# Decay tables as eight rows spread by TensorE, one batch's decays on GpSimd, and fewer products of zeros at the start of a retention and feed-forward kernel

One core of one Trainium2 chip. The metric is the device time of a run in microseconds; the profile's span is 1.7 to 2.1 us shorter than that time in every run here. "Fast": a run within 1.5% of the fastest of its kernel. In the profiles PE is TensorE, PEld its weight loads, DVE VectorE, ACT ScalarE, POOL GpSimd, and SP the engine that issues the loads; a load has landed when its last byte has.

## The reference

```python
def _attn_ref(q, k, v):                       # batch 4, heads 8, sequence 768, head size 64
    gamma = 1.0 - 2.0 ** (-5.0 - np.arange(H, dtype=np.float32))
    scale = 1.0 / np.sqrt(D)
    for t in range(S):
        state = gamma[None, :, None, None] * state + np.einsum('bhd,bhe->bhde', k[:, :, t], v[:, :, t])
        y[:, :, t] = scale * np.einsum('bhd,bhde->bhe', q[:, :, t], state)

def _moe_ref(x, w_in, w_out):                 # 3072 x 512, w_in 512 x 2048, w_out 2048 x 512
    h = x @ w_in
    g = np.maximum(0.01 * h, h)
    return (g @ w_out).astype(np.float32)
```

The recurrence is done in chunks of 128 tokens (per chunk and batch: scores, mask, values, state). The decays of the heads come from a table that the host makes from the number of heads alone. The weights arrive as 64-bit floats in pieces of 512 KB, and ScalarE and VectorE turn each into fp32 before TensorE can use it.

## The kernel before

Only the opening matters here. The table lies in `dec`: 512 columns for the outputs (`gq`), 8 for the values (`gk`), 4 for the states (`gc`), all for 128 partitions.

```python
    dec = const.tile([128, HP * C + H + HP], FP32, name="dec")
    # ...
    def decay_v(c, b, engine=nc.gpsimd):          # values times gk
    def tokens_taken(c, b, xb):                   # outputs times gq, from PSUM into x; taken calls it
    # ...
    load_qk(0, 0)
    nc.sync.dma_start(out=dec[:, rates:], in_=decay[:, rates:])     # 6 KB in rows of 48 bytes
    load_v(0, 0)
    load_qk(0, 1)
    nc.sync.dma_start(out=dec[:, :rates], in_=decay[:, :rates])     # 256 KB
    load_v(0, 1)
    load_piece(0)                                 # first weight piece
    load_qk(0, 2)
    load_v(0, 2)
    load_piece(1)                                 # second weight piece
    # ...
    keep_busy(7)                                  # products of zeros, 128x128 by 128x512
    score(0, 0)
    masked(0, 0)
    decay_v(0, 0, nc.vector)
    keep_busy(6)
    score(0, 1)
    values(0, 0)
    masked(0, 1)
    decay_v(0, 1, nc.vector)
    keep_busy(3)
    next_powers()                                 # ScalarE's three steps on a weight piece
    taken(0, 0, x)
    values(0, 1)
    taken(0, 1, x)
    next_powers()
    next_mantissas()                              # VectorE's three steps: L339, L341, L343
    score(0, 2)
    keep_busy(3)
    steps = direct(0, 0, x, parts[0][1], 0)       # four steps, one for each weight piece
    next(steps)
    next_mantissas()
    # ...
```

The products of zeros have no use but to keep PE busy until data come.

Of the kernel before, what the change touches and what calls it, by code (L numbers as in the profile page):

```python
# [9 lines left out]
FP32 = mybir.dt.float32  # L10
U32 = mybir.dt.uint32
# [5 lines left out]
ALU = mybir.AluOpType  # L17

C = 128
W = 512  # L20
# [3 lines left out]
def kernel(  # L24
# [35 lines left out]
    nc = tc.nc  # L60
    NC = S // C
    DM = H * D
    HP = H // 2
    NU = DF // 512
    N = B * C // 2
    f64 = weights.dtype == I64
# [4 lines left out]
    psum = ctx.enter_context(  # L71
        tc.tile_pool(name="psum", bufs=2, space=bass.MemoryType.PSUM))

    mask = const.tile([128, 128], FP32, name="mask")
    dec = const.tile([128, HP * C + H + HP], FP32, name="dec")
# [17 lines left out]
    def new_pair(h):  # L93

        pairs = units.setdefault(N_UNITS - 1, [])
        if len(pairs) == h:
            pairs.append(work.tile([128, 2, 2, 256], FP32, tag="raw", bufs=3, name=f"last{h}"))
# [12 lines left out]
    gq = dec[:, 0 : HP * C].rearrange("p (j m t) -> p j m t", j=2, t=C)  # L110
    gk = dec[:, HP * C : HP * C + H]
    gc = dec[:, HP * C + H :]
# [5 lines left out]
    def place_for(c, b, place=None):  # L118

        if place is None:  # L120
            x = work.tile([128, 2, HP, C], FP32, tag="qk", bufs=AHEAD, name=f"qk_{c}_{b}")
            y = work.tile([128, 2, H, D], FP32, tag="kv", bufs=AHEAD, name=f"kv_{c}_{b}")
        else:
            flat = place.rearrange("p i k n -> p (i k n)")
            half = 2 * HP * C
            x = flat[:, 0:half].rearrange("p (s a t) -> p s a t", s=2, a=HP)
            y = flat[:, half : 2 * half].rearrange("p (s h d) -> p s h d", s=2, h=H)
        heads[c, b] = x, y

    def load_qk(c, b):  # L130
        nc.sync.dma_start(out=heads[c, b][0], in_=qk[c, b])
# [7 lines left out]
    def load(c, b, place=None):  # L139
        place_for(c, b, place)  # L140
        load_qk(c, b)
        nc.sync.dma_start(out=heads[c, b][1], in_=kv[c, b])

    def decay_v(c, b, engine=nc.gpsimd):
        v = heads[c, b][1][:, 1]
        if engine is not nc.scalar:
            engine.tensor_tensor(out=v, in0=v, in1=gk.unsqueeze(2).to_broadcast([128, H, D]),
                                 op=ALU.mult)
        else:
            for h in range(H):  # L150
                engine.activation(v[:, h], v[:, h], AF.Identity, scale=gk[:, h : h + 1])
# [3 lines left out]
    def two_banks(name):  # L155
        return psum.tile([128, 2, HP, C], FP32, tag="att", bufs=2, name=name)

    def score(c, b):

        x = heads[c, b][0]  # L160
        ps = scores[c, b] = two_banks(f"ap_{c}_{b}")
        for a in range(HP):
            for u in range(2):
                for j in range(2):
                    nc.tensor.matmul(ps[ts(u, 64), j, a, :], lhsT=x[ts(j, 64), 1, a, ts(u, 64)],  # L165
                                     rhs=x[ts(j, 64), 0, a, :])

    def masked(c, b):
        am = work.tile([128, 2, HP, C], FP32, tag="am", bufs=2, name=f"am_{c}_{b}")
        nc.vector.tensor_tensor(  # L170
            out=am.rearrange("p j a t -> p (j a) t"),
            in0=scores[c, b].rearrange("p j a t -> p (j a) t"),
            in1=mask.unsqueeze(1).to_broadcast([128, H, C]), op=ALU.mult)
        scores[c, b] = am
# [54 lines left out]
    def taken(c, b, xb):  # L229

        tokens_taken(c, b, xb)
        state_taken(c, b)

    def tokens_taken(c, b, xb):
        ps = sums_at[c, b]
        th, o = divmod(b * C, N)
        blocks = xb.rearrange("p (kh th) k n -> p kh th k n", th=2)[:, :, th, :, ds(o, C)]
        nc.vector.tensor_tensor(out=blocks, in0=ps[:, :, 0 : HP // 2, :], in1=gq, op=ALU.mult)  # L238

    def state_taken(c, b):  # L240
        ps = sums_at.pop((c, b))
        if 0 < c < NC - 1:
            nc.vector.tensor_tensor(out=st[b], in0=st[b], in1=for_state(ps), op=ALU.add)
            nc.vector.tensor_tensor(out=st[b], in0=st[b],
                                    in1=gc.unsqueeze(2).to_broadcast([128, HP, D]), op=ALU.mult)
# [17 lines left out]
    raws = {}  # L263
# [5 lines left out]
    def piece(n):  # L269

        k, h, i = n // 4, n // 2 % 2, n % 2
        if k < N_UNITS - 1:
            return unit(k)[:, 2 * h : 2 * h + 2, i, :]
        new_pair(h)
        return units[k][h][:, :, i, :]

    def load_piece(n, place=None):
        if n >= N_PIECES:
            return
        if not f64:  # L280
            nc.sync.dma_start(out=piece(n), in_=weights[n].rearrange("p (h n) -> p h n", h=2))
            return
        if place is None:
            tag, bufs = ("raw", 3) if n < N_PIECES - 4 else (("qk", "kv")[n % 2], AHEAD)
            raws[n] = work.tile([128, W], I64, tag=tag, bufs=bufs, name=f"raw{n}")
        else:
            raws[n] = place.bitcast(I64)
        nc.sync.dma_start(out=raws[n], in_=weights[n])
# [4 lines left out]
        if n < N_PIECES and f64:  # L293
            powers(n)

    def next_mantissas():
        n = done["mantissas"]
        done["mantissas"] += 1
        if f64:
            mantissas(n)  # L300
        if n != 3:
            load_piece(n + 4 if n < 3 else n + 3)
        if n == N_PIECES - 1:
            new_pair(2)
            for b in range(AHEAD):
                load(2, b)
        if n % 4 == 3 and n > 7:
            add_sums(n // 4)

    def round_piece():  # L310

        next_mantissas()
        next_powers()
# [17 lines left out]

    def mantissas(n):

        z = zs.pop(n)
        words = raws.pop(n).bitcast(U32).rearrange("p (h n two) -> p h n two", two=2, h=2)
        lo, hi = words[:, :, :, 0], words[:, :, :, 1]
        f = piece(n)
        m = f.bitcast(U32)
        nc.vector.tensor_scalar(out=m, in0=hi, scalar1=0x000FFFFF, scalar2=0x00100000,  # L339
                                op0=ALU.bitwise_and, op1=ALU.bitwise_or)  # L340
        nc.vector.scalar_tensor_tensor(out=f, in0=lo, scalar=2.0 ** -32, in1=m,  # L341
                                       op0=ALU.mult, op1=ALU.add)
        nc.vector.scalar_tensor_tensor(out=f, in0=f, scalar=2.0 ** -20, in1=z.bitcast(BF16),  # L343
                                       op0=ALU.mult, op1=ALU.mult)
# [175 lines left out]
    def tile_x(c):  # L520
        return work.tile([128, 4, 2, N], FP32, tag="x", bufs=2, name=f"x_{c}")

    def new_x(c):
        x = tile_x(c)
        t = work.tile([128, 3, 2, N], FP32, tag="t", bufs=2, name=f"t_{c}")
        return x, t

    def new_o(c):
        return work.tile([128, 4, 2, N], FP32, tag="o", bufs=2, name=f"o_{c}")
# [35 lines left out]
    def rounds(*steps):  # L565
        return {i: [round_piece] for i in steps}

    rates = HP * C
    place_for(0, 0)
    place_for(0, 1)  # L570
    place_for(0, 2, new_o("in2"))
    place_for(0, 3, new_o("in3"))
    load_qk(0, 0)
    nc.sync.dma_start(out=dec[:, rates:], in_=decay[:, rates:])
    load_v(0, 0)
    load_qk(0, 1)
    nc.sync.dma_start(out=dec[:, :rates], in_=decay[:, :rates])
    load_v(0, 1)
    load_piece(0)
    load_qk(0, 2)  # L580
    load_v(0, 2)
    load_piece(1)
    load_piece(2)
    load_piece(3, tile_x("words").rearrange("p i k n -> p (i k n)")[:, 0 : 2 * W])
    load_qk(0, 3)
    load_v(0, 3)
    for b in range(B):
# [6 lines left out]



    xs = {0: new_x(0)}
    os = {}
    parts = [new_g(0, 0)]
    x, t = xs[0]  # L600



# [4 lines left out]
    def keep_busy(n):  # L608
        for _ in range(n):
            nc.tensor.matmul(idle.rearrange("p i n -> p (i n)"), lhsT=nothing[:, 0:128],  # L610
                             rhs=nothing, start=True, stop=True, skip_group_check=True)

    keep_busy(7)
    score(0, 0)
    masked(0, 0)
    decay_v(0, 0, nc.vector)
    keep_busy(6)
    score(0, 1)
    values(0, 0)
    masked(0, 1)  # L620
    decay_v(0, 1, nc.vector)
    keep_busy(3)
    next_powers()
    taken(0, 0, x)
    values(0, 1)
    taken(0, 1, x)
    next_powers()
    next_mantissas()
    score(0, 2)
    keep_busy(3)  # L630
    steps = direct(0, 0, x, parts[0][1], 0)
# [121 lines left out]
def _decay(H, D):  # L753



    import numpy as np

    lg = np.log1p(-(2.0 ** (-5.0 - np.arange(H))))
    t = np.arange(1, C + 1)  # L760
    gq = np.exp(lg[:, None] * t[None, :]) / math.sqrt(D)
    gq = gq.reshape(H // 4, 2, 2, C).transpose(1, 2, 0, 3).reshape(2, -1)
    gc = np.exp(C * lg).reshape(H // 2, 2).T
    return np.concatenate(
        [np.repeat(gq, 64, axis=0), np.exp(-t[:, None] * lg[None, :]), np.repeat(gc, 64, axis=0)],
        axis=1).astype(np.float32)


def _layout(q, k, v, w_in, w_out):
# [60 lines left out]
```

## Time and profile before

| | before |
|---|---|
| time, first three runs | 669.23 us median (668.95 to 669.81) |
| span of the profiled run | 667.9 us (its time 669.81) |
| PE busy | 660.5 us, 99% |
| second weight piece landed | 14.90 us |
| first direct product starts | 16.00 us |
| second piece's product starts | 18.29 us |

An engine that is busy for 99% of the span can't gain much from its own work being shifted about. The one way to shorten such a kernel by shifting is to let the unbroken run start earlier, so the table gives the times of the opening. PE's own timeline there (start, us, engine, line, operation; in brackets the idle time before it and what ended that):

```profile
6.41 1.67 PE L610 MATMUL idle<-t 128*128 128x512 bf16 x6
9.13 1.10 PE L165 MATMUL ap<-qk 64*64 64x128 f32 x32 [1.06 <-DMA qk<-in_qk_dram]
...
16.00 1.99 PE L420 MATMUL d<-x,w 128*128 128x256 f32 x8 [0.85 <-DVE w L343]
18.29 1.99 PE L420 MATMUL d<-x,w 128*128 128x256 f32 x8 [0.29 <-DVE w L343]
```

Here the zeros end before the second queries land. The other lines stand in the prediction. In them "PE d L420 <- DVE w L343: 1.1, 2, 0.9" reads: PE's products named d, of line 420, waited for VectorE's result w of line 343, 1.1 us in total, twice, 0.9 us at the longest.

### The profile page before, as it was taken

Reading aid. Unit: us, or ns where it says so; the run is one execution under the profiler, and the core shown is the slowest. Engines: PE = TensorE matmul, PEld = TensorE weight load, DVE = VectorE, ACT = ScalarE, POOL = GpSimd, SP = SyncE. Lnnn points to the kernel's source line nnn. Section 1 sums busy time; section 2 is a strip of 40 time slices with the busy share of each in tenths; the row PEclk is TensorE's granted clock in tenths of the full one; section 3 lists DMA queues with packets and bytes.
Section 4 is the critical chain, followed back from the end, with each engine's and each line's share of the span. In section 5 each row is a group of like instructions: output and inputs, shape, how many; then the busy total and the mean of one; then the engine's idle time right before and its main releaser. Section 6 shows DMA issues by size and latency. Waiting matters only on the chain.

```text
span 667.9 us, 10403 instructions
## 1 busy us (share of the span) xinstructions
PE 660.5 (99%) x4507; PEld 573.1 (86%) x4507; DVE 371.9 (56%) x570; ACT 175.5 (26%) x321; POOL 19.6 (3%) x21
## 2 busy tenths in 40 slices
PE   7999999999999999999999999999999999999998
PEld 4888888888888888888888888888888888888886
DVE  4789869889889685314542613653531444341342
ACT  2864456255261002111201310210211220221210
POOL 0000000000000111000000100100100000000000
PEclk9999999999999999999999999999999999999999
DMA  8931322322421553003002200301300000000001
GB/s 320 405 113 32 121 69 64 98 92 65 157 64 65 189 190 127 1 0 104 25 16 82 93 1 1 127 1 64 127 1 0 2 0 33 31 1 1 0 1 63
DMA packets 16029, 49.17 MB, mean 74 GB/s; under 512 B 1904, under 2 KB 2160, under 8 KB 15984
## 3 DMA queue, kind: packets, MB, share of 16 engines
q1 hardware_dynamic: 15984, 48.51, 20.9%
q8 instruction: 35, 0.57, 0.3%
q14 instruction: 10, 0.08, 0.0%
HBM read 42.21 MB, written 6.29 MB: 73 GB/s over the span
## 4 chain that ended last, share of the span: by engine, by line
PE 97%; DMA 1%; SPq 1%; DVE 1%; ACT 0%; issue 0%; DVEq 0%
PE B_o L398 12%; PE A_o L398 12%; PE C_o L398 12%; PE C_h L398 12%; PE B_h L398 12%; PE A_h L398 12%; PE D_o L398 6%; PE D_h L398 6%; PE yp L193 3%; PE ap L165 3%; PE d L420 2%; PE yp L184 2%; DMA raw<-in_weights_dram 1%; PE yp L208 1%; PE sums L208 0%; SPq L134 0%
## 5 line engine op out<-in xcount | busy, mean ns | idle before, releaser
L398 PE MATMUL A_h<-x,w 128*128 128x256 f32 x368 | 86.9, 379 | 0.0
L398 PEld LDWEIGHTS A_h<-x,w 128*128 128x128 f32 x368 | 69.9, 190 | 9.5
L398 PE MATMUL A_o<-g,w 128*128 128x256 f32 x288 | 68.0, 379 | 0.0
L433 ACT ACTIVATE g<-g 128x512 f32<-128x512 f32 x69 | 42.0, 630 | 89.3 <-DVE g L347 89.3
L398 PEld LDWEIGHTS A_o<-g,w 128*128 128x128 f32 x288 | 54.7, 190 | 7.4
L438 ACT COPY m<-A_h 128x512 f32<-128x512 f32 x23 | 13.4, 583 | 141.2 <-PE A_h L398 101.6
L347 DVE TENSOR_TENSOR m<-m,B_h 128x512 f32<-128x512 f32 x23 | 15.7, 685 | 57.7 <-PE B_h L398 57.7
L347 DVE TENSOR_TENSOR m<-m,B_o 128x512 f32<-128x512 f32 x16 | 10.9, 684 | 63.9 <-PE B_o L398 63.9
L398 PE MATMUL C_h<-t,w 128*128 128x256 f32 x184 | 44.1, 382 | 0.0
L398 PE MATMUL B_h<-x,w 128*128 128x256 f32 x184 | 44.1, 382 | 0.0
L238 DVE TENSOR_TENSOR x<-yp,dec 128x512 f32<-128x512 f32 x24 | 16.4, 688 | 48.6 <-PE yp L208 34.2
L398 PE MATMUL B_h<-t,w 128*128 128x256 f32 x184 | 43.5, 379 | 0.0
L398 PE MATMUL C_h<-x,w 128*128 128x256 f32 x184 | 43.5, 379 | 0.0
L398 PE MATMUL D_h<-t,w 128*128 128x256 f32 x184 | 43.5, 379 | 0.0
L398 PEld LDWEIGHTS C_h<-t,w 128*128 128x128 f32 x184 | 34.5, 190 | 5.5 <-issue 0.9
L398 PEld LDWEIGHTS D_h<-t,w 128*128 128x128 f32 x184 | 35.0, 190 | 4.8
L398 PEld LDWEIGHTS C_h<-x,w 128*128 128x128 f32 x184 | 35.0, 190 | 4.8
L398 PEld LDWEIGHTS B_h<-t,w 128*128 128x128 f32 x184 | 35.0, 190 | 4.8
L398 PEld LDWEIGHTS B_h<-x,w 128*128 128x128 f32 x184 | 34.5, 190 | 5.1 <-issue 0.3
L350 DVE TENSOR_TENSOR gd<-g,gd 128x512 f32<-128x512 f32 x48 | 34.7, 722 | 1.6
L170 DVE TENSOR_TENSOR am<-ap,mask 128x1024 f32<-128x1024 f32 x24 | 28.5, 1219 | 12.0 <-PE ap L165 12.0
L398 PE MATMUL D_o<-gd,w 128*128 128x256 f32 x144 | 34.0, 379 | 0.0
(110 smaller groups left out, 1018.8 us busy)
## 6 DMA issues: line engine op xcount, KB each, us to landing
raw<-in_weights_dram SPq DMA_DIRECT2D x31, 512.0 KB, 4.0
qk<-in_qk_dram SPq DMA_DIRECT2D x19, 512.0 KB, 3.6
kv<-in_kv_dram SPq DMA_DIRECT2D x17, 512.0 KB, 4.6
out_dram<-o SPq DMA_DIRECT2D x23, 256.0 KB, 2.1
in<-in_qk_dram SPq DMA_DIRECT2D x3, 512.0 KB, 7.2
in<-in_kv_dram SPq DMA_DIRECT2D x3, 512.0 KB, 7.8
kv<-in_kv_dram SPq DMA_DIRECT2D x4, 256.0 KB, 7.5
o_in<-in_qk_dram SPq DMA_DIRECT2D x2, 512.0 KB, 9.0
```

Of the source, the lines that this page charges most:

```text
L165: nc.tensor.matmul(ps[ts(u, 64), j, a, :], lhsT=x[ts(j, 64), 1, a, ts(u, 64)], rhs=x[ts(j, 64), 0, a, :])
L170: nc.vector.tensor_tensor(out=am.rearrange("p j a t -> p (j a) t"), in0=scores[c, b].rearrange("p j a t -> p (j a) t"), in1=mask.unsqueeze ...
L184: nc.tensor.matmul(ps[ts(i, 64), j, m, :], lhsT=st[b][ts(j, 64), a, :], rhs=x[ts(j, 64), 0, a, :], start=(m == 0), stop=False, skip_group_ ...
L193: nc.tensor.matmul(ps[ts(i, 64), j, m, :], lhsT=y[:, 1, 2 * a + j, :], rhs=am[:, j, a, :], start=(c == 0 and m == 0), stop=True, skip_grou ...
L208: nc.tensor.matmul(sp[ts(j, 64), a, :], lhsT=y[:, 0, 2 * a + j, :], rhs=y[:, 1, 2 * a + j, :], start=start, stop=True, skip_group_check=True)
L238: nc.vector.tensor_tensor(out=blocks, in0=ps[:, :, 0 : HP // 2, :], in1=gq, op=ALU.mult)
L347: nc.vector.tensor_tensor(out=out, in0=a, in1=b, op=ALU.add)
L350: nc.vector.tensor_tensor(out=out, in0=a, in1=b, op=ALU.subtract)
L398: nc.tensor.matmul(half, lhsT=block(w, sa)[:, k, ts(i, 128)], rhs=rhs[:, k, :], start=(first and (i == 0 or split) and n == 0 and k == 0), ...
L420: nc.tensor.matmul(banks[r][:, i, :], lhsT=block(2 * u, r + 2 * kh)[:, k, ts(i, 128)], rhs=x[:, 2 * kh + th, k, :], start=(step == 0 and i ...
L433: nc.scalar.activation(g[:, i], g[:, i], AF.Prelu, alpha=0.01)
L438: nc.scalar.copy(out=got["m1"], in_=ps)
```

## The change

Its intent: get 237 KB of table out of the way of the weights by sending eight rows and letting TensorE spread them over the partitions, in a stretch where it multiplied zeros; take work off VectorE ahead of the first direct product.

```diff
+    rows = t[0:H, 1:3].rearrange("p i k n -> p (i k n)")[:, 0 : decay.shape[1]]
+    nc.scalar.dma_start(out=rows, in_=decay)
     load_qk(0, 0)
-    nc.sync.dma_start(out=dec[:, rates:], in_=decay[:, rates:])
     load_v(0, 0)
     load_qk(0, 1)
-    nc.sync.dma_start(out=dec[:, :rates], in_=decay[:, :rates])
     load_v(0, 1)
 ...
     score(0, 0)
+    nc.tensor.matmul(tables[:, 0, 0:H], lhsT=by_head, rhs=ones, start=True, ...)
+    nc.tensor.matmul(tables[:, 0, H : H + HP], lhsT=place, rhs=g_c, start=False, ...)
     masked(0, 0)
+    nc.vector.tensor_copy(out=dec[:, n_gq:], in_=tables[:, 0, 0 : H + HP])
+    nc.tensor.matmul(spread.rearrange("p i n -> p (i n)"), lhsT=place, rhs=g_q, start=True, ...)
+    nc.scalar.copy(out=dec[:, 0:n_gq], in_=spread.rearrange("p i n -> p (i n)"))
     decay_v(0, 0, nc.vector)
-    keep_busy(6)
     score(0, 1)
     values(0, 0)
     masked(0, 1)
-    decay_v(0, 1, nc.vector)
-    keep_busy(3)
+    decay_v(0, 1)                       # GpSimd
+    keep_busy(1)
     next_powers()
     taken(0, 0, x)
     values(0, 1)
-    taken(0, 1, x)
+    next_mantissas(lambda: taken(0, 1, x))      # upper bits, outputs, then the rest
     next_powers()
-    next_mantissas()
```

(`by_head`, `ones`, `place`, `g_q` and `g_c` are parts of the eight rows: the decays of the values with a unit matrix that turns them over, and the other decays with rows of ones that say which half of the partitions gets which row.)

More of the change, by code (lines that the diff above doesn't have):

```diff
@@ L294, in next_powers, with next_mantissas @@
             powers(n)
-    def next_mantissas():
+    def next_mantissas(between=None):
         n = done["mantissas"]
         done["mantissas"] += 1
-        if f64:
+        if f64 and between is None:
             mantissas(n)
+        elif f64:
+            mantissas_upper(n)
+            between()
+            mantissas_rest(n)
+        elif between is not None:
+            between()
         if n != 3:
@@ L332, in mantissas, with mantissas_upper, mantissas_rest @@
     def mantissas(n):
+        mantissas_upper(n)
+        mantissas_rest(n)
+    def mantissas_upper(n):
+        hi = raws[n].bitcast(U32).rearrange("p (h n two) -> p h n two", two=2, h=2)[:, :, :, 1]
+        nc.vector.tensor_scalar(out=piece(n).bitcast(U32), in0=hi, scalar1=0x000FFFFF,
+                                scalar2=0x00100000, op0=ALU.bitwise_and, op1=ALU.bitwise_or)
+    def mantissas_rest(n):
         z = zs.pop(n)
         words = raws.pop(n).bitcast(U32).rearrange("p (h n two) -> p h n two", two=2, h=2)
-        lo, hi = words[:, :, :, 0], words[:, :, :, 1]
+        lo = words[:, :, :, 0]
         f = piece(n)
         m = f.bitcast(U32)
-        nc.vector.tensor_scalar(out=m, in0=hi, scalar1=0x000FFFFF, scalar2=0x00100000,
-                                op0=ALU.bitwise_and, op1=ALU.bitwise_or)
         nc.vector.scalar_tensor_tensor(out=f, in0=lo, scalar=2.0 ** -32, in1=m,
@@ L566, in rounds @@
         return {i: [round_piece] for i in steps}
-    rates = HP * C
     place_for(0, 0)
@@ L572 @@
     place_for(0, 3, new_o("in3"))
+    words = tile_x("words").rearrange("p i k n -> p (i k n)")[:, 0 : 2 * W]
+    xs = {0: new_x(0)}
+    x, t = xs[0]
+    rows = t[0:H, 1:3].rearrange("p i k n -> p (i k n)")[:, 0 : decay.shape[1]]
+    nc.scalar.dma_start(out=rows, in_=decay)
     load_qk(0, 0)
-    nc.sync.dma_start(out=dec[:, rates:], in_=decay[:, rates:])
     load_v(0, 0)
     load_qk(0, 1)
-    nc.sync.dma_start(out=dec[:, :rates], in_=decay[:, :rates])
     load_v(0, 1)
@@ L583 @@
     load_piece(2)
-    load_piece(3, tile_x("words").rearrange("p i k n -> p (i k n)")[:, 0 : 2 * W])
+    load_piece(3, words)
     load_qk(0, 3)
@@ L593 @@
                             base=0, pattern=[[1, 128]], channel_multiplier=-1)
-    xs = {0: new_x(0)}
     os = {}
     parts = [new_g(0, 0)]
-    x, t = xs[0]
     nothing = t[:, 0, 0, :].bitcast(BF16)
@@ L611, in keep_busy @@
                              rhs=nothing, start=True, stop=True, skip_group_check=True)
+    tables = psum.tile([128, 2, N], FP32, tag="ff", bufs=4, name="tables")
+    spread = psum.tile([128, 2, N], FP32, tag="ff", bufs=4, name="spread")
+    n_gq = HP * C
+    ends = [0, C, C + H, 2 * C + H, 2 * C + H + n_gq, 2 * C + H + n_gq + HP]
+    by_head, ones, place, g_q, g_c = (rows[:, i:j] for i, j in zip(ends, ends[1:]))
     keep_busy(7)
     score(0, 0)
+    nc.tensor.matmul(tables[:, 0, 0:H], lhsT=by_head, rhs=ones, start=True, stop=True,
+                     skip_group_check=True)
+    nc.tensor.matmul(tables[:, 0, H : H + HP], lhsT=place, rhs=g_c, start=False, stop=True,
+                     skip_group_check=True)
     masked(0, 0)
+    nc.vector.tensor_copy(out=dec[:, n_gq:], in_=tables[:, 0, 0 : H + HP])
+    nc.tensor.matmul(spread.rearrange("p i n -> p (i n)"), lhsT=place, rhs=g_q, start=True,
+                     stop=True, skip_group_check=True)
+    nc.scalar.copy(out=dec[:, 0:n_gq], in_=spread.rearrange("p i n -> p (i n)"))
     decay_v(0, 0, nc.vector)
-    keep_busy(6)
     score(0, 1)
@@ L763, in _decay @@
     gc = np.exp(C * lg).reshape(H // 2, 2).T
-    return np.concatenate(
-        [np.repeat(gq, 64, axis=0), np.exp(-t[:, None] * lg[None, :]), np.repeat(gc, 64, axis=0)],
-        axis=1).astype(np.float32)
+    place = np.concatenate([np.repeat(np.eye(2), 64, axis=1), gq, gc], axis=1)
+    place = np.concatenate([place, np.zeros((H - 2, place.shape[1]))])
+    return np.concatenate([np.exp(-lg[:, None] * t[None, :]), np.eye(H), place],
+                          axis=1).astype(np.float32)
 def _layout(q, k, v, w_in, w_out):
```

## The prediction

> **What bounds the kernel now.** I read the page first, then the waits of PE after the opening, then the chain that ended last, then the timeline of the first 30 us and the stretches of DMA. The page says where the time is:
>
> ```profile
> PE 660.5 (99%) x4507; PEld 573.1 (86%) x4507; DVE 371.9 (56%) x570; ACT 175.5 (26%) x321; POOL 19.6 (3%) x21
> PE 97%; DMA 1%; SPq 1%; DVE 1%; ACT 0%; issue 0%; DVEq 0%
> ```
>
> PE is busy for 99% of the 667.9 us and is 97% of the chain. All that the change touches lies in the first 16 us or so. So the question is when PE enters its unbroken run, and whether that moment moves. All waits of PE from 16 us to the end are these:
>
> ```profile
> PE d L420 <- DVE w L343: 1.1, 2, 0.9
> PE yp L184 <- DVE am L170: 0.5, 1, 0.5
> ```
>
> Two of the three are waits of the direct products d for a weight piece that DVE has just finished; the second of these ends at 18.29 us. From there PE loses only the 0.5 us near 43 us, which follows PE's own scores and moves with them. Whatever moves 18.29 us moves the end of the kernel by as much. The chain in order of time tells what sets 18.29:
>
> ```profile
> 4.67 1.01 SPq L134
> 5.72 9.18 DMA raw<-in_weights_dram
> 14.93 0.67 ACT w L327
> 15.62 0.64 ACT z L329
> 16.28 0.44 DVE w L339
> 16.74 0.70 DVE w L341
> 17.54 0.70 DVE w L343
> 18.29 1.99 PE d L420 x8
> ```
>
> The second weight piece (issued at 5.72) lands at 14.90. ACT works on it for 1.3 us until DVE may start, DVE finishes it in three instructions, and 18.29 - 14.90 = 3.39 us after the landing PE multiplies by it. PE and DVE before 14.9 us aren't on this chain. The chain hangs on the DMA, and the stretches show the DMA full (columns: PE, PEld, DVE, ACT and POOL busy, clock, DMA share, GB/s):
>
> ```profile
> 4.00:5.00 1.00, 1.00 (x14) 0.51 (x16) 0.00 (x0) 0.00 (x0) 0.00 (x0) 1.00 0.78 217
> 5.00:6.00 1.00, 1.00 (x24) 1.00 (x22) 0.00 (x0) 0.00 (x0) 0.00 (x0) 1.00 0.73 250
> 9.00:10.00 1.00, 0.87 (x32) 0.86 (x32) 0.00 (x0) 0.00 (x0) 0.00 (x0) 1.00 1.03 418
> 12.00:13.00 1.00, 0.74 (x15) 0.76 (x16) 0.73 (x2) 0.97 (x2) 0.00 (x0) 1.00 1.03 412
> ```
>
> From 7 us on all engines of the DMA are busy at about 410 GB/s; between 4 and 7 us they move only 217 to 295 GB/s. Among what goes ahead of the second weight piece are the two transfers of the decay table:
>
> ```profile
> dec<-decay_dram SPq DMA_DIRECT2D x1, 256.0 KB, 7.1
> dec<-decay_dram SPq DMA_DIRECT2D x1, 6.0 KB, 3.2
> ```
>
> **What the Trainium skill says.** "DMA: Bandwidth & Descriptors", section Queues, rings and completion order: the SP and ACT queues have a ring each on the same 16 engines, and each engine takes its descriptors in ring order. The trace of before agrees for the order on SP: the landings come in the order of issue (first queries at 4.3, second batch's at 9.1, first weights at 11.7, second at 14.9), so bytes taken out ahead come off everything behind. "SBUF — State Buffer", section Who interferes with whom: a VectorE instruction with two SBUF inputs contends with a GpSimd instruction that reads SBUF, and the one that issues second blocks. The trace has the GpSimd decay multiplication 16 times at 1042 to 1524 ns (mean 1191) against 682 on DVE; no wait in it shows such a block by itself. "TensorE: Matmul & The Clock Gate", section Part 1: the clock halves after an idle window of about 3.4 us, and such a window's busy stretch restores it. The trace agrees with a slow start: the first seven products of zeros take 3.17 us (0.45 each), the six after the first scores 1.67 (0.28 each). "ScalarE: Activation LUTs", section Table sets: copy is in every set. The trace agrees, with one table load for Prelu, Relu, Identity and Copy together, so I expect no second load for the new ScalarE copy.
>
> **The change part by part.**
>
> (1) The table: 256 KB and 6 KB on SP go, and 8 rows of 3120 B (25 KB) come on ACT's queue. Bytes on the rings ahead of the weights: 262 - 25 = 237 KB, or 0.58 us at 410 GB/s. The 6 KB were 128 packets of 48 B and cost more than their bytes, and the new rows use a part of the engines only while the first queries still come; I take 0.65 us off every landing behind. This part is on the path.
>
> (2) Two SP issues of 0.47 us (0.43 and the gap) go: first values are issued 0.47 earlier, the second batch's queries also 0.47, the first weights 0.94. From 7 us on the DMA is full and an earlier issue gives nothing. Between 4 and 7 us there are 3 x 410 - 762 = 468 KB of unused room, 1.1 us; if a part of that comes from the many issues of small size, it's won. I can't see why those packets are slow and count 0.2 us. Beside it, eight transfers are in flight at most (the twelfth waited for the fourth), with two fewer on the list the issues of weights two to four wait for earlier landings, a further hint in the same direction.
>
> (3) PE: three small products and one of 8 rows by 512 columns, 0.43 us at full clock by the 128x256 products (1.73 us for eight, so 0.216 each) and double that when slow. They run at 6.4 to 7.3 us, in the place of six products of zeros that ran to 8.08, while PE has nothing to do until the second queries land at about 9. Off the path. The rows should land at about 4 us (the 6 KB transfer took 3.2 us from issue), before the first scores end at 6.4.
>
> (4) DVE: a copy of 128x12 from PSUM, some 0.1 to 0.2 us, is added before the first decays; 0.68 us of the second batch's decays go to GpSimd. ACT: one copy of 128x512, 0.58 us, near 7.5 us where ACT sits idle until 11.72. GpSimd starts when the second values land (10.4 before, some 9.8 after) and ends by about 11, before the mask of the second batch ends at 11.5. In that time DVE runs the mask, with one operand in PSUM, so the two don't meet.
>
> (5) The first weight piece: its first DVE step goes between the two decays of outputs. Reckoned anew with unchanged queries at 9.1: second mask to 11.5, first outputs to 12.2, the upper bits at 12.4 (after ACT's second step on a piece that lands at 11.05) to 12.9, second outputs to 13.5, the two others to 15.0. The first direct product then starts at about 15.0 instead of 16.00. That doesn't reach the end: PE then waits for the second piece instead, some 0.6 us where it waited 0.29.
>
> Sum: the second piece lands at 14.90 - 0.65 - 0.2 = 14.05, plus the unchanged 3.39 gives 17.44 for its product, in place of 18.29: 0.85 us. ACT's and DVE's work after it hangs on the same landing, with PE only 0.17 us behind DVE at the third piece (weight load at 22.27), so it moves as one block. From 50 to 660 us PE is busy 610.00 of 610 us and nothing there changes. 669.23 - 0.85 = 668.4 us.
>
> **The rivals.** *Start of the DMA*: the slow stretch at 4 to 7 us comes of the two added transfers, of their 48-byte packets or of the place in the queue. Then the second piece comes 1.5 us or more earlier. For it speaks that the share of the DMA is under 0.85 only there; against it that the slow packets are those of queries and values, which stay. DVE then becomes the next limit: it can't start the second piece before about 14.7 to 15.0, which caps the gain near 1.6 us: 667.6 us. *Clock of PE*: with eight products of zeros fewer, PE idles from 7.3 to 9 and between the second batch's steps; if the clock halves there, scores and values of the second batch take 2 us each in place of 1.1 and the first direct products 4 in place of 2. That eats the gain and may give 669.3 to 670. Against it: the idle time is some 1.7 us, half the window named above, where it was 1.06 before. *Wait exchanged*: the table becomes late, because the rows, their products and the copies are now in series before the first decays. By (3) and (4) it's ready at about 8 us and the decays end at 8.7 instead of 8.44, still before the second scores; it'd take over 1 us more to reach the path. *GpSimd blocks DVE*: up to 1.2 us once, with slack of 0.3 to 1 us on DVE's side before the second piece; at worst no gain, 669.2.
>
> **Range and chances.** The three runs before spread from 668.95 to 669.81, so 0.4 us is noise to either side. Gain 0.85 with the start rival on one side (a chance of 0.25) and clock or blocks on the other (0.15) gives 667.4 to 669.2. Two per cent are 13.4 us; the whole stretch that changes is 18 us long and PE works in most of it, so faster or slower by that much needs something that nobody sees in this profile: 0.01 each, and 0.98 for within.
>
> **What would show it right or wrong.** In the profile after: the landing of the second weight piece near 14.05 (the ACT instruction on it starts then) and its direct product near 17.4; the first direct product at about 15.0, with a gap of PE behind it; one table load on ACT; the product of 512 columns done before 7.5; the scores of the second batch in 1.1 us, which excludes the clock rival; GpSimd's 1.2 us before 11.2. PE busy falls by some 2 us with the zeros, without use for the span. The prediction is wrong if that product starts later than 18 us or earlier than 16.5, or if the run of PE after it has new gaps.

## The result, and the profile after

Six runs of each kernel: 668.05 us after (667.48 to 668.81), 668.93 us before (668.84 to 669.81). Ratio 0.9985, interval 0.9972 to 0.9998. A ratio here is the mean time of one kernel's fast runs over that of the other's of the same rounds, so it isn't quite the ratio of the medians. That is 0.88 us less by the medians.

The chain of the kernel after, in order of time (start, us, what):

```profile
5.08 8.12 DMA raw<-in_weights_dram
...
13.22 0.67 ACT w L334
...
14.58 0.44 DVE w L346
...
16.59 1.99 PE d L434 x8
```

The second weight piece lands at 13.20 in place of 14.90, and its product starts at 16.59 in place of 18.29: again 3.39 us after the landing. The span falls from 667.9 to 666.3 us. PE's waits and its page line, after:

```profile
PE d L434 <- DVE w L357: 1.4, 2, 1.0
PE yp L184 <- DVE am L170: 0.5, 1, 0.5
```

```profile
PE 659.5 (99%) x4505; PEld 572.8 (86%) x4505; DVE 374.3 (56%) x570; ACT 176.0 (26%) x322; POOL 20.1 (3%) x22
```

The waits are the same two, and behind 50 us nothing changed. The two traces differ by 1.7 us, though, and the medians by 0.88. That contradiction is the first thing to settle. PE's timeline in the opening, after (start, us, engine, line, operation):

```profile
4.62 1.43 PE L165 MATMUL ap<-qk 64*64 64x128 f32 x32
...
6.44 1.10 PE L642 MATMUL spread<-t 8*128 8x512 f32 x2
7.76 1.10 PE L165 MATMUL ap<-qk 64*64 64x128 f32 x32 [0.22 <-DMA qk<-in_qk_dram]
...
13.58 1.99 PE L434 MATMUL d<-x,w 128*128 128x256 f32 x8 [0.39 <-DVE w L357]
16.59 1.99 PE L434 MATMUL d<-x,w 128*128 128x256 f32 x8 [1.01 <-DVE w L357]
```

The spreading product fills the time until the second queries land, the second scores take 1.10 us, and PE has 1.01 us to spare before the second piece's product.

### The profile page after: what moved, and what is told of

It is laid out like the page before. It is cut to its first block, busy times and chain, and to the rows that moved or that the text cites. A ratio compares the mean times of both kernels' runs of the same rounds, so it can differ in the third digit from the quotient of the medians.

```text
span 666.3 us, 10403 instructions
## 1 busy us (share of the span) xinstructions
PE 659.5 (99%) x4505; PEld 572.8 (86%) x4505; DVE 374.3 (56%) x570; ACT 176.0 (26%) x322; POOL 20.1 (3%) x22
## 4 chain that ended last, share of the span: by engine, by line
PE 97%; DMA 1%; SPq 1%; DVE 1%; ACT 0%; issue 0%; DVEq 0%
PE B_o L412 12%; PE A_o L412 12%; PE C_o L412 12%; PE C_h L412 12%; PE B_h L412 12%; PE A_h L412 12%; PE D_o L412 6%; PE D_h L412 6%; PE yp L193 3%; PE ap L165 3%; PE d L434 2%; PE yp L184 2%; DMA raw<-in_weights_dram 1%; PE yp L208 1%; SPq L134 0%; PE sums L208 0%
## 5 line engine op out<-in xcount | busy, mean ns | idle before, releaser
L412 PE MATMUL B_o<-gd,w 128*128 128x256 f32 x144 | 34.0, 379 | 0.0
```

The lines of the kernel that those rows point to most:

```text
L412: nc.tensor.matmul(half, lhsT=block(w, sa)[:, k, ts(i, 128)], rhs=rhs[:, k, :], start=(first and (i == 0 or split) and n == 0 and k == 0), ...
```

## The experiments

My theory: the landing of the second weight piece sets the start of PE's unbroken run, and the 256 KB that are gone set the landing. Rivals: the start of the DMA (many issues, 48-byte packets); PE's and VectorE's own chain; the clock of PE. Twelve kernels ran. All were correct. "Ratio" is to the kernel before. The third column is when the second piece's product starts in the profiled run.

| run | median us (range) | its product at | piece landed | ratio |
|---|---|---|---|---|
| e1 before again | 668.98 (668.18 to 669.59) | 17.45 | 14.07 | 0.9997 |
| e2 table only | 669.34 (668.98 to 673.08) | 17.64 | 12.74 | 1.0013 |
| e3 rest only | 669.08 (668.47 to 670.57) | 18.41 | 13.81 | 1.0004 |
| e4 with 256 KB | 668.47 (668.14 to 670.59) | 16.95 | 13.56 | 0.9998 |
| e5 after again | 669.04 (667.54 to 670.53) | 19.16 | 12.66 | 1.0002 |
| e6 zeros back | 668.37 (667.98 to 668.90) | 17.00 | 12.95 | 0.9991 |
| e7 DVE decays | 668.13 (667.36 to 668.80) | 16.57 | 13.11 | 0.9988 |
| e8 piece first | 667.28 (667.08 to 667.61) | 15.84 | 12.44 | 0.9976 |
| e9 rest, warm | 668.82 (668.53 to 669.63) | 16.99 | 13.59 | 1.0000 |
| e10 two small | 668.41 (668.12 to 670.46) | 19.02 | 12.98 | 0.9997 |
| e11 cold start | 671.03 (670.51 to 671.09) | 19.64 | 12.68 | 1.0028 |
| e12 piece first again | 667.43 (666.85 to 668.28) | 16.02 | 12.63 | 0.9976 |

(Where the two direct products run as one group of 16, the second's start is worked out as the first's plus 1.92 us, the time of eight such products; in e8 and e12 it is read from the chain.) Span minus that start is 649.5 to 649.7 us in all twelve, and in the two first traces too (667.9 - 18.29 and 666.3 - 16.59). So everything behind this product is a block of fixed length, and each experiment can be read from the product's start. That helps, because the times of equal kernels scatter by a microsecond, more than most effects sought here.

**e1, the kernel before unchanged.**

> The kernel before, unchanged, for a second trace. The profiled run of before was the slowest of its six (669.81 against a median of 668.93), and there the second weight piece landed at 14.90 us. If that run had an unlucky start of the DMA, this trace shows the landing near 14.0 to 14.3 and the product of that piece near 17.4 to 17.7, with the time within 0.1% of the other runs of before. The rival (a start of the DMA that is always this slow in the kernel before, so that the change is worth the 1.7 us between the two traces) expects 14.7 to 15.0 again. Ratio 1.000 either way.

The chain of this trace:

```profile
5.69 8.37 DMA raw<-in_weights_dram
...
14.09 0.68 ACT w L327
...
17.45 1.99 PE d L420 x8
```

The piece landed at 14.07, and the run's time, 668.98, is the median of its five. So the first trace of before (669.81) was of an unlucky run, but a slow start of its DMA it was not: up to 7 us it had moved 1.39 MB, here 1.29. The loads up to and with the second piece are 3.68 MB. When it landed, the DMA had moved 4.63 MB there and 4.19 here, so more of the loads issued behind it had gone first: 0.44 MB, 1.1 us at 410 GB/s. Why is open. Against this trace the change is worth 17.45 - 16.59 = 0.86 us, which agrees with the medians. The contradiction was one of which run got profiled.

**e2, the table alone.** Zeros, VectorE's decays and the order of the first piece as before:

```diff
     decay_v(0, 0, nc.vector)
+    keep_busy(6)
     score(0, 1)
 ...
-    decay_v(0, 1)
-    keep_busy(1)
+    decay_v(0, 1, nc.vector)
+    keep_busy(3)
 ...
-    next_mantissas(lambda: taken(0, 1, x))
+    taken(0, 1, x)
     next_powers()
+    next_mantissas()
```

> The change with its other parts undone: eight rows and their spreading by PE, but the products of zeros (6 and 3), the second batch's decays on DVE and the order of the first weight piece as before. My theory (what counts is the landing of the second piece, moved by the 237 KB that are gone): the whole gain, 668.0 to 668.2 us, ratio to before 0.9985 to 0.9989. Rival (DVE's and PE's work before the second piece counts): under half of the gain, 668.5 or more.

No gain: my theory falls in the form I gave it. The piece landed at 12.74, so 3.39 us later its product could have started at 16.13. PE's timeline shows what came instead:

```profile
7.45 1.47 PE L624 MATMUL idle<-t 128*128 128x512 bf16 x6
8.84 1.10 PE L165 MATMUL ap<-qk 64*64 64x128 f32 x32
...
15.72 3.86 PE L434 MATMUL d<-x,w 128*128 128x256 f32 x16 [0.86 <-DVE w L357]
```

The second queries had landed at 7.38. The six products of zeros, now behind the spreading product, held the second scores until 8.84; masks, VectorE's decays and outputs followed, and the first direct product started at 15.72 and the second right behind it, without a wait for the piece. With the landing earlier, the chain through PE and VectorE was the later of the two. (One run of 673.08 us in this set I can't explain.)

**e3, the rest alone.** The kernel before with GpSimd's decays, the split order and few zeros, the old table kept. (The zeros are six and two fewer; the expectation says five.)

```diff
-    keep_busy(6)
     score(0, 1)
 ...
-    decay_v(0, 1, nc.vector)
-    keep_busy(3)
+    decay_v(0, 1)
+    keep_busy(1)
 ...
-    taken(0, 1, x)
+    next_mantissas(lambda: taken(0, 1, x))
     next_powers()
-    next_mantissas()
```

> The kernel before with only the other parts: the decay table of 262 KB as before, but the second batch's decays on GpSimd, the upper bits of the first piece ahead and five plus two products of zeros fewer. My theory: the first direct product starts earlier, by 0.5 us or more, PE then waits longer for the second piece, and the time is that of before within 0.2 us (ratio 0.9997 to 1.0003). Rival: 0.4 us or more of gain.

No gain in time, but not by the way I expected. The piece landed at 13.81, so its product could have started at 17.20; it started at 18.41:

```profile
4.49 1.99 PE L165 MATMUL ap<-qk 64*64 64x128 f32 x32
8.01 1.98 PE L165 MATMUL ap<-qk 64*64 64x128 f32 x32 [1.53 <-DMA qk<-in_qk_dram]
...
16.49 3.85 PE L434 MATMUL d<-x,w 128*128 128x256 f32 x16 [0.41 <-DVE w L357]
```

The second scores took 1.98 us, as long as the first, in place of 1.10. In every trace the products at the start take about twice their later time (the first seven zeros 0.45 us each; in e2, from 7.45 us, 0.25) and go over to full pace at some moment. I read that as a halved clock and call the moment its release. Here it came only after the second values (1.93 us at 12.37). That is the clock rival of the prediction, though not by its mechanism: the clock wasn't lost in the idle 1.53 us, the first scores were slow already.

**e4, 256 KB put back** on SP into a tile that isn't in use yet:

```diff
     load_qk(0, 1)
+    nc.sync.dma_start(out=spare, in_=qk[0, 3][:, 0])     # 256 KB, unused
     load_v(0, 1)
```

> The kernel after with one load of 256 KB, whose data nothing uses, put back on the SP queue at the place of the old table. My theory: it costs what its bytes take at 410 GB/s, 0.64 us, so about 668.7 us, ratio to before near 0.9997. Rival (the number of issues, the 48-byte packets or the start of the DMA was what counted): under 0.3 us, so 668.3 or less.

The piece landed at 13.56. The six traces with the new table and the old order of loads (after, e2, e5, e6, e7, e11) have 12.66 to 13.20, mean 12.89. By the mean the bytes cost 0.67 us, where 0.64 was reckoned; it is one trace against six that scatter by 0.54, so 0.4 to 0.9 us. The product started at 16.95, 0.36 later than in the first trace of after. The times can't resolve this: the ratio to before is 0.9998 with the interval 0.9984 to 1.0012.

**e5, the kernel after unchanged.**

> The kernel after, unchanged, as the measure for the other runs of this call and for a second trace. My theory: second weight piece landed at 12.9 to 13.5, its product 3.4 us later at 16.3 to 16.9; scores of the second batch in 1.1 us (clock not halved); time 0.6 to 1.1 us under before, ratio 0.9984 to 0.9991.

A surprise: three runs at 667.54, 667.79 and 668.12 us, three at 669.95, 670.45 and 670.53. The profiled run is of the second kind:

```profile
4.66 1.98 PE L165 MATMUL ap<-qk 64*64 64x128 f32 x32
...
7.45 2.05 PE L642 MATMUL spread<-t 8*128 8x512 f32 x2
9.43 1.99 PE L165 MATMUL ap<-qk 64*64 64x128 f32 x32
...
17.24 3.85 PE L434 MATMUL d<-x,w 128*128 128x256 f32 x16 [0.40 <-DVE w L357]
```

The piece landed early, at 12.66. But the spreading product took 2.05 us (1.10 in the first trace), the second scores 1.99, and the first direct product came at 17.24. PE had worked nearly without pause since 1.39 us and was still at half its pace. The column of the granted clock doesn't show it; this is the stretch from 8 to 10 us, columns as in the prediction:

```profile
8.00:10.00 2.00, 2.00 (x14) 0.57 (x16) 0.78 (x3) 0.47 (x1) 1.54 (x1) 1.00 1.00 400
```

It says 1.00. Only the durations give the slow clock away. The product of the second piece came at 19.16, past the 18 us that the prediction named as its sign of being wrong.

**e6, the zeros put back in the kernel after** (six ahead of the second scores, three ahead of the second values).

```diff
     decay_v(0, 0, nc.vector)
+    keep_busy(6)
     score(0, 1)
 ...
-    keep_busy(1)
+    keep_busy(3)
```

> The kernel after with the products of zeros of before (six ahead of the second scores, three ahead of the second values; six and one, now none and one, so eight more). They stand behind the new spreading product in PE's order and end about 8.9 us, while the second queries land at 7.4 to 7.7. My theory, formed on the trace of the table alone: they delay the second scores by 1.1 us and the first direct product to about 14.7; PE then reaches the second piece's product at about 16.7, so nearly nothing to 0.3 us is lost, because GpSimd and the new order have taken 1 us out of DVE's chain. Rival (removing the zeros is what made the gain): 0.8 us lost, time as before.

The first direct product started at 15.08 and the second piece's at 17.00; the landing (12.95) would have allowed 16.34. So the zeros cost 0.66 us there, twice what I expected at most. None of the five runs was slow (667.98 to 668.90), and their mean, 668.33, is not above the 668.59 of all twelve runs of after: in the times no loss shows.

**e7, VectorE's decays and the first piece in one go, in the kernel after.**

```diff
-    decay_v(0, 1)
+    decay_v(0, 1, nc.vector)
     keep_busy(1)
 ...
-    next_mantissas(lambda: taken(0, 1, x))
+    taken(0, 1, x)
     next_powers()
+    next_mantissas()
```

> The kernel after with the second batch's decays on DVE and the first weight piece's bits in one go, as before; few zeros as in after. My theory: the first direct product starts 0.7 to 1.0 us later (about 14.5), PE is still through with it when the second piece is ready, and the time is that of after within 0.2 us. Rival (DVE's relief counts): 0.5 us or more lost.

As expected: first direct product at 14.65 (13.58 in the first trace of after), second at 16.57 against 16.59. The relief of VectorE is real and nearly all used up in the wait for the piece: without it the chain through PE and VectorE ends last, but by 0.07 us only (the landing at 13.11 allowed 16.50). Median 668.13 us, within 0.1 of after's first six.

**e8 and e12, the second weight piece loaded ahead of the third batch's values** (256 KB).

```diff
     load_qk(0, 2)
-    load_v(0, 2)
     load_piece(1)
+    load_v(0, 2)
```

> The kernel after with the load of the second weight piece ahead of the third batch's values (256 KB) on SP. My theory (the landing of that piece sets the start of PE's unbroken run): it lands 0.65 us earlier, its product starts at about 15.9 to 16.0, and the time falls by 0.5 to 0.7 us under after, to about 667.4. Rival (PE's or DVE's own work binds by then): under 0.2 us.

> The version with the second piece ahead of the third batch's values once more, on another chip if it falls so, to see whether its gain holds: 667.1 to 667.6 in the runs whose clock is released early, ratio to before 0.997 to 0.998. By my theory of the clock up to half of the runs can be 2 to 3 us slower, as in the second trace of after, for it has as few zeros; if none is, the share of such runs stays open.

667.28 and 667.43 us, both ratios 0.9976 with intervals that end at 0.9988 and 0.9989: this version beats the kernel before. It beats after too, by runs of different calls: its ten have a mean of 667.38, the nine of after below 669 us one of 668.01. In e12 the piece lands at 12.63 and its product starts at 16.02, 3.39 us later. In e8 the chain goes through the first piece instead:

```profile
9.89 0.69 ACT w L334
...
11.70 0.69 DVE x L238
...
13.84 1.99 PE d L434 x8
...
15.84 1.99 PE d L434 x8
```

There the first piece's product follows VectorE's work, and the second piece's stands right behind it: the two chains have met, and loading this piece earlier still would give nothing in such a run. None of the ten runs reached 669 us.

**e9, the rest alone with six zeros kept.** As e3, with

```diff
     decay_v(0, 0, nc.vector)
+    keep_busy(6)
     score(0, 1)
```

> The kernel of the third experiment (old table; GpSimd decays, upper bits ahead) with the six products of zeros ahead of the second scores put back. The third one ran with the slow clock from its first product to about 14 us (scores 1.98, values 1.97 us). My theory of the clock: full-array products of zeros at 6.4 to 8 us are what gets the clock released before the second scores, the first scores and an idle PE don't. So here the second scores and values take 1.1 us, the first direct product starts near 14.3 to 15.0, PE waits for the second piece (landing 13.8 to 14.9, product 3.4 us later), and the time is that of before within 0.3 us. Rival (the slow clock there was chance and not the missing zeros, or is DVE's doing): slow scores of 2 us again, or a gain of 0.5 us or more.

```profile
4.49 1.99 PE L165 MATMUL ap<-qk 64*64 64x128 f32 x32
6.41 1.69 PE L624 MATMUL idle<-t 128*128 128x512 bf16 x6
8.03 1.10 PE L165 MATMUL ap<-qk 64*64 64x128 f32 x32
...
16.99 1.99 PE L434 MATMUL d<-x,w 128*128 128x256 f32 x8 [0.75 <-DVE w L357]
```

The second scores take 1.10 us, PE waits 0.75 us for the second piece, the time is that of before (1.0000). In this run the clock was released before the second scores, during the six zeros (1.69 us for them, 1.47 in e2). That they did it is likely and not shown: one trace stands against that of e3, and the two traces of after show that the same kernel can go either way. With the old table the landing is the limit, and the rest of the change has nothing to give.

**e10, two loads of 6 KB** in 48-byte rows put back, on SP, where the table's stood:

```diff
     load_qk(0, 0)
+    nc.sync.dma_start(out=spare[:, 0:12], in_=qk[0, 3][:, 0, 0, 0:12])
     load_v(0, 0)
     load_qk(0, 1)
+    nc.sync.dma_start(out=spare[:, 12:24], in_=qk[0, 3][:, 0, 0, 12:24])
```

(`spare`: a part of a tile not in use yet.)

> The kernel after with two loads of 6 KB in 48-byte rows, whose data nothing uses, on SP at the places where the two table loads stood. The five traces with the new table and the old order of loads have the second piece landed at 12.66 to 13.20 (mean 12.93), the three with the old table at 13.81 to 14.90 (mean 14.26), and the one with 256 KB put back at 13.56. If the number of issues or the 48-byte packets make up the rest (0.7 us), this one lands at 13.3 to 13.6. If only bytes count, 12.7 to 13.1.

The piece landed at 12.98, 0.09 us behind the mean without them. So the number of issues and the small rows don't make up the missing 0.7 us; that rival falls. A cost of 0.2 us or so one trace can't exclude. The profiled run was again one with the slow clock (670.46 us, first scores 1.99, second scores 1.99); the other three took 668.12 to 668.54.

**e11, no zeros at the start.**

```diff
-    keep_busy(7)
     score(0, 0)
```

> The kernel after without the seven products of zeros at the start. My theory: without them the clock isn't released before the second values in any run, so first scores 2 us, spreading product near 2 us, second scores 2 us; the first direct product starts near 17 us and every run takes 670 to 671, as the slow runs of the second trace of after (670.5) did. Rival (the slow runs had another cause, as a slow DMA): time as after in its fast runs, 667.5 to 668.8.

```profile
4.71 1.99 PE L165 MATMUL ap<-qk 64*64 64x128 f32 x32 [4.71 <-DMA qk<-in_qk_dram]
...
9.48 1.98 PE L165 MATMUL ap<-qk 64*64 64x128 f32 x32
...
17.72 3.85 PE L434 MATMUL d<-x,w 128*128 128x256 f32 x16 [0.41 <-DVE w L357]
```

All four runs took 670.51 to 671.09 us, with the piece landed at 12.68. A clock that isn't released by the second scores costs the kernel after 2 to 3 us, and that's the size of the slow runs of e5.

## Why the prediction was right, and where it wasn't

**The landing sets the end: right for the first two traces and e1, incomplete.** In these the product follows the landing by 3.39 us, and the rest is a block of fixed length. But the landing is one of two chains that end there. The other goes through the second scores, the masks and VectorE. In e2 it took over at once, and in e5, the kernel after itself, it put the product 3.11 us behind what the landing allowed. The gain needs both: the table brings the landing forward, and fewer zeros keep the other chain level with it (e7). VectorE's relief with all the zeros does it in part (e6: 17.00, against 17.64 in e2 and 17.45 in e1). Each half alone showed no gain (e2, e3, e9).

**The size: near, and partly by luck.** 0.85 us was predicted, 0.88 is the difference of the medians and 0.86 that of the two traces of middling runs. But 0.2 of it stood for issues, which no run confirms, the landing moved by more than 0.85, and late releases of the clock take some of the gain back in other runs. The absolute time, 668.4 against 668.05, is off by the start: I took 669.23 from three runs, and the later median is 668.93. The traced run of before was the slowest, which I saw in its time and didn't draw the conclusion from: the predicted product at 17.44 came at 16.59, just above the 16.5 at which the prediction would have called itself wrong.

**The bytes: right, as far as one trace tells.** 0.64 us reckoned for the 256 KB, 0.67 measured (e4). **The issues and small rows: not shown.** I gave them 0.2 us; e10 measured 0.09, inside the scatter. The landing moved by more than the bytes: the four traces with the old table have 13.59 to 14.90 (mean 14.09), the six with the new one have a mean of 12.89, so 1.2 us. Without the late first trace it is 0.9. What makes up the rest stays open. Up to 7 us the DMA had moved 1.29, 1.32 and 1.52 MB in e1, e3 and e9 (old table), and 1.43 to 1.71 in the six with the new one, so its start may have a part in it; with both issues put back (e10) it was 1.53.

**"Off the path" for PE, step 3: the failed step.** Its cost was taken too low. The spreading product, reckoned at 0.43 us, took 1.10 (2.05 at half pace): the trace lists each fp32 product twice (a step of `direct` has four in the code and eight in the trace, the spreading one stands there as x2), so the eight that I took at 0.216 are four products of 256 columns, and one of 512 costs 0.86 by the same lines. The three new products (I wrote four) ran from 5.97 to 7.54 us where 6.4 to 7.3 was predicted. In the first trace of after they still ended before the queries landed. But in e2, e5, e7, e10 and e11 they stand on the chain that ended last. Nor did the step hold for the zeros: with queries at 7.4 us (I reckoned with 9.1, from the first trace), the zeros are on the path (e2, e6). And taking them out may cost an early clock.

**The clock rival: right in size of harm, wrong in mechanism and in chance.** I expected the clock to be lost in an idle stretch, and gave 0.15 to clock and blocks together. What happens is that the clock isn't released in time, with PE busy all along (e5). Of the twelve runs of after, three were over 669.9 us; of the 15 runs of e4, e7 and e10, which have as few zeros, two (670.59 and 670.46). Two of these five are traced, and both have slow scores; for the others the clock is inferred from the time. With six zeros ahead of the second scores (e6, e9), none of ten was. But two of the 42 runs of before (670.43 and 670.01) and one of e2 (673.08) were, with as many zeros and no trace, so the time alone doesn't prove a slow clock, and the share of such starts with and without zeros is not settled. Over all, the median of after (12 runs) is 668.10 and its mean 668.59; of before (42 runs, on at least two chips) 668.91 and 668.99. So the mean gains only 0.40 us, which the scatter of the twelve (some 0.7 us to either side) doesn't tell from nothing: the gain of 0.88 is one of the starts with an early clock. That the piece-first version showed none in ten runs may be chance.

**The rest.** One table load on ACT, as the cited page led me to expect. The DVE copy took 0.16 us, the ACT copy 0.58, GpSimd 1.04 us (8.54 to 9.58) without a block of VectorE: all near what was reckoned, off the path in the first trace. The first direct product came at 13.58 and not 15.0, for the second queries came 1.4 us earlier. The rivals of a late table and of VectorE blocked by GpSimd have nothing for them in any trace. The other way round there is something: GpSimd's decays took 1.04 or 1.05 us in eight traces, also beside VectorE's mask, which reads PSUM, but 1.54 in e5 and 1.48 in e11, the two in which they ran beside VectorE's decays, which have both operands in SBUF, for more than half a us (e5: GpSimd from 8.18, VectorE 8.13 to 8.82). There it had slack and cost nothing.

## What to carry to other kernels

When two chains end at the same instruction, count what the second one allows before you pay for shortening the first: here neither half of the change showed a gain alone. The seven products of zeros at the start insure the clock (without them all four runs of e11 were slow); six more later cost 0.66 us on the path in one trace. Judge their removal by many runs, since a single profile can show either state, and by the durations of products, not by the clock column. When you take the cost of a product from a trace, count how often the trace lists it. And ask which of its runs a profile shows: one late landing in the trace of before doubled the apparent gain.

## What the Trainium skill lacked or had wrong

- "TensorE: Matmul & The Clock Gate", Part 1, puts the release some 4 us into sustained matmul activity, 0.5 us more or less. Here (e5) PE ran from 1.39 us to past 13 us with hardly a pause before full pace: 3.17 us of full-array zeros, then products of 64x64 and of 8 rows. In other runs of the same kernel the clock was free during the first scores (1.43 us in place of 1.98). The page doesn't say what such partial products count for; that they count less is my reading and was not tested apart.
- The same page warns that clock events in a profile are unreliable and asks for a cross-check. The runs agree: the clock column gave 1.00 where products took twice their time.
- "DMA: Bandwidth & Descriptors", Specifications, gives 512 B as the smallest transfer for full rate, and not what a few smaller rows cost the loads behind them. Two loads in 48-byte rows (e10) delayed these by 0.09 us, within the scatter.
